# A Fourier mixing stage and routed experts: the final logits matmul as a stream of its own, and block transposes that read the SBUF copy of u one step later

## The chip, the core and the metric

The kernel runs on one core of a Trainium2 chip. The metric is the device time in microseconds of one launch, lower is better. A core has five engines that run side by side, each through its own instructions in program order: TensorE (PE in the profile, with its weight loads as PEld), VectorE (DVE), ScalarE (ACT), GpSimd (POOL) and SyncE (SP), which here issues nearly all DMA transfers. [...] An instruction whose operand is not there yet holds up everything behind it on its engine.

## The reference

Two blocks follow each other. The first is a mixing of 8 sequences of 2496 tokens with 256 channels in frequency space; the second sends each of the 19968 tokens to the one of 8 experts with the largest logit.

```python
X = np.fft.rfft(x, axis=1)                     # x: (8, 2496, 256)
y = np.fft.irfft(X * (filt_r + 1j * filt_i)[None], n=2496, axis=1)

x = y.reshape(19968, 256)
logits = x @ w_gate                            # (256, 8)
expert_idx = np.argmax(logits, axis=1)
probs = np.exp(logits - logits.max(-1, keepdims=True))
probs /= probs.sum(-1, keepdims=True) + 1e-09
gate_w = probs[np.arange(N), expert_idx]
# for each expert e, over its tokens:
h = np.maximum(x_e @ w1[e], 0.0)               # (256, 1024)
y_e = h @ w2[e]                                # (1024, 256)
out = gate_w[:, None] * y
```

## The kernel before, in words

**The transform.** 2496 = 39 x 64, so the transform of a sequence (a "batch" here) is taken as a two-dimensional one, by matmuls with tables. Of the 39 frequencies along the first axis 20 are kept, as real and imaginary parts. There are four stages. Stage A (line 361) takes the 39-point transform of `x` into `zd` in DRAM. Stage B (line 375) takes the 64-point transform; VectorE multiplies its product by the filter (lines 382 to 384) and adds the two halves (line 388 on GpSimd or 391 on VectorE). Stage C (line 401) takes the inverse 64-point transform, giving `u`, which goes to `ud` in DRAM. Stage D (line 423) takes the inverse 39-point one, giving the tokens `yo`. Stages A and D run in six chunks of up to four columns, B and C in ten pairs of frequencies. Between the stages the data are rearranged by the trip through DRAM: the stores are `zd<-zo` and `ud<-uo`, the loads `fin<-zd` (line 346), `fin<-ud` (line 353) and `fin<-in_x` (line 341). A load takes one of seven `fin` buffers.

**The logits.** They are taken from `u`, ahead of stage D, since stage D acts on another axis than the gate. In before, stage C's product in PSUM is read twice: a copy to SBUF (`uo`, line 402, on VectorE or ScalarE) for the trip through DRAM, and a transpose of 32 x 32 blocks on VectorE (line 406) into `tu`. For each of two halves of the frequencies (12 and 8) `u_logits` multiplies `tu` by the gate (line 525, 32 small matmuls), and `turn_logits` turns the result (line 551) and stores it to `vd` in DRAM in four pieces. After the second half `load_logits` brings it back into `spec` in six pieces (line 566), and `logits` applies the last 39-point transform to it (line 575). Only after this matmul does the routing of the batch start: `route` works out expert and row of each token on VectorE, `send_rows` scatters the tokens' rows to DRAM by GpSimd, and `tile_map` finds which tile of rows belongs to which expert. The first batch takes another way through on-chip transposes and has no trip of its logits through DRAM.

**The experts.** Tiles of 512, 256 or 128 rows of one expert are loaded (`xg<-rows`, line 775, and `ng`, 779), turned on VectorE (line 814), multiplied by `w1` (line 857 in a form that saves an eighth of the products, line 898 plainly) and by `w2` (line 915), and scattered to the output (line 921). The weights `w1t` and `w2t` are loaded in halves of 512 KB (lines 808 and 804). Row number and expert are read by SP from values that VectorE wrote.

**What sets the order.** PE, VectorE, ScalarE and SP stand in an order that the Python code works out itself. `slot(k)` lists the steps of a time slot: stages B and C of batch k, stage A of batch k + 1, stage D and the routing of batch k - 1. Each step is a tuple of a due time as a share of the slot, the function, the data that it needs, a charge in microseconds of PE, and a stream: "b", "a" or "d". The main loop keeps a clock, `now`, moved on by the charges. It takes the first step of the list; if that one's data are reckoned to be late by this clock (`lands`), it looks among the next 16 steps for the first ready one, but passes over every step of a stream of which an earlier step has been passed over. Between steps of the transform it gives out expert work, by a credit. After each step the stores noted one step earlier are issued (`flush`), delayed loads whose time has come are issued, and further loads follow (`more_loads`, `prefetch`). The clock only orders the instructions; on the chip each engine waits for its semaphores.

For the last logits matmul the clock works so: `turn_logits` of the second half sets the load to 5.0 after `now`, `load_logits` reckons the landing at 7.0 after the issue, and `logits(k - 1)` is a step of stream "d", ahead of the six chunks of stage D of that batch.

```python
delayed.append((now[0] + 5.0, lambda: load_logits(b)))          # line 557
lands["v", b] = now[0] + 7.0                                    # line 570
steps.append((at - 0.04, lambda: logits(k - 1), ("v", k - 1), 0.3, "d"))   # line 967
```

`free["v"]` and `free["s"]` are the planner's guess of when VectorE and ScalarE come free; `either` sends a copy to the one that would be done first.

Of the kernel before, what the change touches and what calls it, by code (L numbers as in the profile page):

```python
# [10 lines left out]
F32 = mybir.dt.float32  # L11
# [8 lines left out]
P = 128  # L20
S = 2496
D = 256
# [98 lines left out]
def kernel(  # L121
# [16 lines left out]
    nc = tc.nc  # L138
# [9 lines left out]
    for b in range(B):  # L148
        GROUPS.append([])
        for rows, most in WANT[b]:  # L150
            n = min(most, max(0, ((b + 1) * S - (N - left) - E * (rows - 1)) // rows))
# [32 lines left out]
    sb = fft.enter_context(tc.tile_pool(name="sb", bufs=2))  # L184
# [38 lines left out]
    now = [0.0]  # L223
# [22 lines left out]
    HALVES = [(0, 12), (12, NF - 12)]  # L246
# [121 lines left out]
    def stage_b(b, f):  # L368
        c, j = divmod(f, 4)
        if b == 0:  # L370
            zi, j = outs.pop(("zi", f)), 0
        else:
            zi = ins["z", b, c] if j == 0 else ins.pop(("z", b, c))
        p = bank()
        mm(p, lhsT=tbs, rhs=zi[:, j:j + 2, :], start=True, stop=True)  # L375

        z2 = p.rearrange("p (i d) -> p i d", i=2)
        ys = outs["y", b, f] = sb.tile([P, 2, D], F32, tag="ys", name="ys", bufs=4)
        yw = (pro if b == 0 else sb).tile([P, 2, D], F32, tag="yw", name="yw", bufs=2)
        half, f1 = divmod(f, NF // 2)  # L380
        fi = ht[half * HP:(half + 1) * HP, NF + f1:NF + f1 + 2, :]
        nc.vector.tensor_mul(ys, z2, ht[:, f:f + 2, :])  # L382
        nc.vector.scalar_tensor_tensor(out=yw[:HP], in0=z2[HP:], scalar=-1.0, in1=fi, op0=ALU.mult, op1=ALU.mult)
        nc.vector.tensor_mul(yw[HP:], z2[:HP], fi)
        free["v"] = max(free["v"], now[0]) + 2.1

        if b == 0 or b < 3 and not sides:
            nc.gpsimd.tensor_tensor(ys, ys, yw, op=ALU.add)
            free["p"] = max(free["p"], free["v"]) + (1.4 if b else 0.0)
        else:  # L390
            nc.vector.tensor_tensor(ys, ys, yw, op=ALU.add)
            free["v"] += 0.7

    def stage_c(b, f):
        ys = outs.pop(("y", b, f))
        j = f % 4
        if j == 0:
            outs["u", b] = sb.tile([P, 4, D], F32, tag="st", name="uo", bufs=4)
        uo = outs["u", b]
        p = bank()  # L400
        mm(p, lhsT=tcs, rhs=ys, start=True, stop=True)  # L401
        evac(uo[:, j:j + 2, :], p.rearrange("p (i d) -> p i d", i=2), 512)
        f0, n = HALVES[f >= HALVES[0][1]]
        if f == f0:
            outs["t", b] = sb.tile([P, HALVES[0][1], D], F32, tag="tu", name="tu", bufs=1)
        nc.vector.transpose(outs["t", b][:, f - f0:f - f0 + 2, :].rearrange("p i d -> p (i d)"), p)  # L406
        free["v"] = max(free["v"], now[0]) + 0.7
        if j == 2:
            f0 = f - 2
            move(ud[b][:, f0:f0 + 4, :], uo[:HP])  # L410
            move(ud[b][:, NF + f0:NF + f0 + 4, :], uo[HP:])
        if f == NF - 2:
            mark(("c", b))
# [116 lines left out]
    def turn_logits(b, half=0):  # L530
        ls = outs.pop(("l", b))
        if b == 0:
            for i0, m in ((0, 4), (4, 2)):
                pt = bank().rearrange("p (i w) -> p i w", i=4)
                for i in range(m):
                    nc.tensor.transpose(pt[:TK, i, :], ls[:, i0 + i, :], ident)
                pv = pt[:TK].rearrange("p i (g c) -> p i g c", g=4)
                for i in range(m):
                    c = 4 * (i0 + i)
                    w = min(4, NG - c)  # L540
                    whole = min(w, NG - 1 - c)
                    evac(spec[0][:, c:c + whole], pv[:, i, :whole, :E], 8 * whole)
                    if whole < w:
                        evac(spec[0][:NS, c + whole:c + w], pv[:NS, i, whole:w, :E], 8)
            lands["v", b] = now[0]
            return
        f0, n = HALVES[half]
        w = n // 4 * CT
        pt = bank()[:w, :P]
        vt = sb.tile([HALVES[0][1] // 4 * CT, P], F32, tag="vt", name="vt", bufs=1)[:w]  # L550
        nc.tensor.transpose(pt, ls, ident)
        evac(vt, pt, P)
        for m in range(4):
            move(vd[b][m, f0:f0 + n].rearrange("(g k) r e -> (k r) g e", g=4),
                 vt.rearrange("p (g m e) -> p m g e", g=4, m=4)[:, m])
        if half:
            delayed.append((now[0] + 5.0, lambda: load_logits(b)))

    def load_logits(b):
        for th in range(2):  # L560
            of = vd[b][2 * th:2 * th + 2].rearrange("c f r e -> (c f) r e")
            for j in range(NB):
                i0 = -((j - th * HT) // NB) if th else 0
                t0 = NB * i0 + j - th * HT
                n = (HT - 1 - t0) // NB + 1
                nc.sync.dma_start(
                    out=spec[b % 2][j * NS:(j + 1) * NS, i0:i0 + n],
                    in_=of[:, t0:t0 + NB * (n - 1) + 1:NB, :],
                )
        lands["v", b] = now[0] + 7.0  # L570

    def logits(b):
        lgs[b] = sb.tile([TP, NG, E], F32, tag="lg", name="lg", bufs=1)
        p = bank()[:TP, :NG * E]
        mm(p, lhsT=tds, rhs=spec[b % 2].rearrange("p i e -> p (i e)"), start=True, stop=True)
        evac(lgs[b].rearrange("p i e -> p (i e)"), p, NG * E)
        sides.append(route(b))
# [355 lines left out]
    def slot(k):  # L933

        steps, nch = [], len(CH)
        if k == 0:
            steps.append((0.4, load_rest, None, 0.0, None))
            for f in range(-2, NF + 2, 2):
                at = (f + 2) / (NF + 4)
                if 0 <= f < NF:  # L940
                    steps.append((at, lambda f=f: stage_b(k, f), None, 0.85, "b"))
                if f + 2 < NF:
                    steps.append((at + 0.01, lambda f=f: turn_z(f + 2), None, 0.44, "b"))
                if f >= 2:
                    steps.append((at + 0.02, lambda f=f: first_c(f - 2), None, 0.85, "b"))
        elif k < B:
            for f in range(0, NF + 4, 2):
                at = f / (NF + 4)
                if f < NF:
                    steps.append((at, lambda f=f: stage_b(k, f), ("z", k, f // 4) if f % 4 == 0 else None, 0.85, "b"))  # L950
                if f >= 4:
                    steps.append((at + 0.01, lambda f=f: stage_c(k, f - 4), None, 0.85, "b"))
            for half, (f0, n) in enumerate(HALVES):
                at = (f0 + n + 4) / (NF + 4) + 0.005
                steps.append((at, lambda half=half: u_logits(k, half), None, 2.6 if half == 0 else 2.1, "b"))
                steps.append((at + 0.04, lambda half=half: turn_logits(k, half), None, 0.2, "b"))
        if k + 1 < B:
            for c in range(nch):
                steps.append(((0.25 if k == 0 else 0.0) + 0.7 * c / nch, lambda c=c: stage_a(k + 1, c), ("x", k + 1, c), 0.43 * CH[c][1], "a"))
        if k > 0:  # L960
            for c in range(nch + 1):
                at = 0.8 * c / (nch + 3) - 0.1 if k == 1 else (0.35 if k == 2 else 0.2) + 0.8 * c / (nch + 3)
                if c == 0:
                    if k == 1:
                        steps.append((at - 0.07, lambda: u_logits(k - 1), None, 4.4, "d"))
                        steps.append((at - 0.06, lambda: turn_logits(k - 1), None, 0.7, "d"))
                    steps.append((at - 0.04, lambda: logits(k - 1), ("v", k - 1), 0.3, "d"))
                if c < nch and k == 1:
                    steps.append((at - 0.05, lambda c=c: turn_u(c), None, 0.22 * CH[c][1], "d"))
                if c < nch:  # L970
                    steps.append((at, lambda c=c: stage_d(k - 1, c), ("u", k - 1, c) if k > 1 else "y", 0.43 * CH[c][1], "d"))
                    steps.append((at + 0.02, lambda c=c: sides.append(send_rows(k - 1, c)), None, 0.0, "d"))
                if k == 1 and c == nch:
                    steps.append((at, experts_pool, None, 0.0, "d"))
            steps.append((0.73 if k == 1 else 2.0, lambda: begin_route(k - 1), None, 0.0, "d"))
        return sorted(steps, key=lambda step: step[0])
# [249 lines left out]
```

## Time and profile before

| what | us |
|---|---|
| median of three runs | 1525.34 (1522.54 to 1527.35) |
| the profiled execution | 1525.43 |
| its span, first to last instruction | 1523.7 |
| PE busy | 1430.0 |
| PE weight loads busy | 1131.9 |
| VectorE busy | 741.5 |
| GpSimd busy | 702.4 |
| ScalarE busy | 444.3 |
| data moved | 278.01 MB, 182 GB/s in the mean |

The profile was taken in one execution. In it busy times are unions of an engine's instructions; the difference to the span is time in which the engine waited. In lists of waits a line reads: engine, what it was about to do, what it waited for, then the total in us, how often, and the longest. In windows the columns are the stretch, then for PE, PEld, DVE, ACT and POOL the busy us with the number of instructions, then the granted clock of TensorE, the mean busy share of the 16 DMA engines, and GB/s. In a timeline a line is start, duration, engine, source line, operation, what is written and read, and how many are merged, with the idle time before it in brackets. A matmul of the program shows as two records. Groups of instructions end with busy us, mean ns of one, and the engine's idle time before them with what ended it. SPq is SP's queue, in which a DMA shows with the time that its issue took.

### The profile page before, as it was taken

What the parts mean: (1) busy time and instruction counts of PE and PEld (TensorE: products, weight loads), DVE (VectorE), ACT (ScalarE), POOL (GpSimd) and SP (SyncE); (2) the same over time, 40 slices, a digit from 0 to 9 for tenths busy, and PEclk for the clock granted to TensorE, in tenths of its full rate; (3) what the DMA queues carried; (4) which work ended last, traced back from release to release, by engine and by line L of the source; (5) the groups of instructions that cost most, each with busy time, mean ns of one, the idle gap of its engine ahead of it and who ended that gap; (6) DMA issues with size and microseconds to landing.
All of it is one profiled execution on the core that took longest, in us unless ns stands there. A gap on an engine that the chain in (4) does not pass through costs nothing. (4 is left out here: it accounts for less than half of the span.)

```text
span 1523.7 us, 23874 instructions
## 1 busy us (share of the span) xinstructions
PE 1430.0 (94%) x7354; PEld 1131.9 (74%) x7354; DVE 741.5 (49%) x1479; ACT 444.3 (29%) x870; POOL 702.4 (46%) x911
## 2 busy tenths in 40 slices
PE   7986967999999997999989996999999999999998
PEld 5533525766777776777857885788888889999997
DVE  4684675264766555555577454446525343440000
ACT  3531422233232222222212222222222222224332
POOL 3351616325445641566427543566455546741111
PEclk9997988999999998999999998999999999999999
DMA  9788988889877648765486437453655453455661
GB/s 222 195 245 237 270 216 270 232 222 325 230 197 216 188 138 195 190 182 162 129 174 191 132 116 179 116 157 96 207 171 189 144 174 103 119 188 171 186 185 40
DMA packets 253416, 278.01 MB, mean 182 GB/s; under 512 B 162471, under 2 KB 200752, under 8 KB 253289
## 3 DMA queue, kind: packets, MB, share of 16 engines
q1 hardware_dynamic: 234169, 233.13, 56.0%
q0 software_dynamic: 19120, 43.33, 8.5%
q8 instruction: 62, 1.02, 0.3%
q14 instruction: 65, 0.53, 0.1%
HBM read 195.80 MB, written 81.22 MB: 182 GB/s over the span
## 5 line engine op out<-in xcount | busy, mean ns | idle before, releaser
L915 PE MATMUL bank<-w2t,hT 128*128 128x256 f32 x1984 | 443.7, 381 | 0.4 <-ACT hT L870 0.4
L861 DVE TENSOR_TENSOR hT<-bank,hT 128x512 f32<-128x512 f32 (+1 forms) x504 | 298.9, 626 | 283.2 <-PE bank L857 189.3
L915 PEld LDWEIGHTS bank<-w2t,hT 128*128 128x128 f32 x1984 | 378.1, 191 | 69.2 <-issue 15.0
L921 POOL DMA_INDIRECT out_dram<-ys,ng x161 | 160.4, 996 | 479.3 <-DMA out_dram<-ys,ng 138.1
L865 ACT ACTIVATE hT<-hT 128x1024 f32<-128x1024 f32 (+1 forms) x144 | 131.9, 955 | 340.0 <-DVE hT L861 340.0
L681 POOL DMA_INDIRECT rows<-yo,row x176 | 179.4, 1019 | 76.5 <-issue 46.7
L857 PE MATMUL bank<-xT,w1t 128*128 128x256 f32 (+1 forms) x864 | 190.0, 356 | 0.0
L920 ACT ACTIVATE ys<-bank,ng 128x256 f32<-128x256 f32 x136 | 64.3, 473 | 407.5 <-PE bank L915 324.0
L857 PEld LDWEIGHTS bank<-xT,w1t 128*128 128x128 f32 x864 | 152.3, 190 | 25.2 <-issue 6.5
L857 PE MATMUL bank<-sums,wsum 128*128 128x256 f32 (+1 forms) x576 | 135.1, 357 | 1.1 <-POOL sums L821 0.8
L915 PE MATMUL bank<-w2s,hT 128*128 x592 | 132.6, 379 | 0.0
L898 PEld LDWEIGHTS bank<-xT,w1t 128*128 128x128 f32 x864 | 116.1, 193 | 18.9 <-issue 12.5
L898 PE MATMUL bank<-xT,w1t 128*128 128x128 f32 (+1 forms) x864 | 125.8, 301 | 2.7 <-DVE xT L814 2.7
L814 DVE STREAM_TRANSPOSE xT<-xg 128x512 f32<-128x512 f32 (+2 forms) x126 | 57.4, 493 | 142.0 <-PE bank L898 122.4
L915 PEld LDWEIGHTS bank<-w2s,hT 128*128 128x128 f32 x592 | 110.3, 190 | 13.8
L857 PEld LDWEIGHTS bank<-sums,wsum 128*128 128x128 f32 x576 | 101.4, 190 | 23.9 <-issue 9.9
L382 DVE TENSOR_TENSOR ys<-bank,ht 128x512 f32<-128x512 f32 x80 | 54.7, 684 | 91.5 <-PE bank L375 91.1
L361 PE MATMUL bank<-fin,tas 117*120 117x512 f32 x154 | 76.9, 620 | 10.8 <-DMA fin<-in_x_dram 10.8
L832 POOL TENSOR_TENSOR wsum<-w1t 128x256 f32<-128x256 f32 x72 | 53.5, 744 | 69.2 <-PE bank L857 44.4
L904 ACT ACTIVATE hT<-bank 128x128 f32<-128x128 f32 (+1 forms) x209 | 62.6, 300 | 55.0 <-PE bank L898 49.8
L401 PE MATMUL bank<-ys,tcs 128*128 128x512 f32 x140 | 73.5, 611 | 4.9 <-DVE ef L726 3.1
L406 DVE STREAM_TRANSPOSE tu<-bank 128x512 f32<-128x512 f32 x70 | 49.4, 709 | 57.1 <-ACT uo L238 56.6
(157 smaller groups left out, 1496.3 us busy)
## 6 DMA issues: line engine op xcount, KB each, us to landing
w1t<-in_moe_w_dram SPq DMA_DIRECT2D x126, 512.0 KB
w2t<-in_moe_w_dram SPq DMA_DIRECT2D x68, 512.0 KB
fin<-in_x_dram SPq DMA_DIRECT2D x39, 512.0 KB
fin<-zd SPq DMA_DIRECT2D x70, 256.0 KB
ud<-uo SPq DMA_DIRECT2D x70, 256.0 KB
zd<-zo SPq DMA_DIRECT2D x35, 480.0 KB
fin<-ud SPq DMA_DIRECT2D x35, 480.0 KB
xg<-rows SPq DMA_DIRECT2D x112, 128.0 KB
```

The source lines that it names most:

```text
L361: mm(p[:TK, :], lhsT=tas, rhs=xt[:TP, j:j + 2, :], start=True, stop=True)
L401: mm(p, lhsT=tcs, rhs=ys, start=True, stop=True)
L681: sc = nc.gpsimd.indirect_dma_start(out=rowsd, out_offset=bass.IndirectOffsetOnAxis(ap=at, axis=0), in_=what, in_offset=None,)
L814: nc.vector.transpose(xts[i][:, dh, :n * P].rearrange("p (g r) -> p g r", r=QW), xg[:, :n * NQ, dh, :])
L857: mm(q[:, v], lhsT=left[:, v * P:(v + 1) * P], rhs=right, start=True, stop=True)
L861: nc.vector.tensor_tensor(o, q, a, op=ALU.add)
L865: nc.scalar.activation(o.rearrange("p v r c -> p v (r c)"), q.rearrange("p v r c -> p v (r c)"), AF.Relu)
L898: mm(p[:, :m], lhsT=w1t[2 * i + g][:, dh, fh, v * P:(v + 1) * P], rhs=xts[i][:, dh, :m], start=(dh == 0), stop=(dh == DH - 1))
L904: lambda: nc.scalar.activation(hT, p[:, :m], AF.Relu))
L915: mm(p[:, :D], lhsT=hs[i][k % 4 // 2][:, k // 4, k % 2, j * P:(j + 1) * P], rhs=w2, start=(k == 0), stop=(k == FT - 1))
L920: lambda: nc.scalar.activation(ys, p[:, :D], AF.Copy, scale=gate))
L921: nc.gpsimd.indirect_dma_start(out=out, out_offset=bass.IndirectOffsetOnAxis(ap=gis[i].bitcast(U32)[:, j, :1], axis=0), in_=ys, in_offset= ...
```

## The change

Three things are changed.

Stage C no longer transposes its product out of PSUM. It notes the pair of frequencies in a list, and a new function, `turn_u_blocks`, transposes what is on the list from `uo` in SBUF. It is called by the next stage C before its matmul, by stage B between its products and its add, and as a step of its own shortly before each `u_logits`.

The charges of `u_logits` in the planner are lowered: 2.6 and 2.1 to 1.5 and 1.1 for the two halves, and 4.4 to 2.4 for the first batch.

The final logits matmul becomes stream "l", so that a passed-over `logits` doesn't keep back stage D; its load is delayed by 6.0 instead of 5.0, and its landing is reckoned at 10.0 instead of 7.0 after the issue.

```diff
@@ stage_b
         nc.vector.tensor_mul(yw[HP:], z2[:HP], fi)
+        turn_u_blocks()
         free["v"] = max(free["v"], now[0]) + 2.1
@@
+    turns = []
+
+    def turn_u_blocks():
+
+        for b, f, u in turns:
+            f0, n = HALVES[f >= HALVES[0][1]]
+            if f == f0:
+                outs["t", b] = sb.tile([P, HALVES[0][1], D], F32, tag="tu", name="tu", bufs=1)
+            nc.vector.transpose(outs["t", b][:, f - f0:f - f0 + 2, :].rearrange("p i d -> p (i d)"),
+                                u.rearrange("p i d -> p (i d)"))
+            free["v"] = max(free["v"], now[0]) + 0.6
+        turns.clear()
+
     def stage_c(b, f):
         ys = outs.pop(("y", b, f))
+        turn_u_blocks()
         j = f % 4
...
         evac(uo[:, j:j + 2, :], p.rearrange("p (i d) -> p i d", i=2), 512)
-        f0, n = HALVES[f >= HALVES[0][1]]
-        if f == f0:
-            outs["t", b] = sb.tile([P, HALVES[0][1], D], F32, tag="tu", name="tu", bufs=1)
-        nc.vector.transpose(outs["t", b][:, f - f0:f - f0 + 2, :].rearrange("p i d -> p (i d)"), p)
-        free["v"] = max(free["v"], now[0]) + 0.7
+        turns.append((b, f, uo[:, j:j + 2, :]))
@@ turn_logits
         if half:
-            delayed.append((now[0] + 5.0, lambda: load_logits(b)))
+            delayed.append((now[0] + 6.0, lambda: load_logits(b)))
@@ load_logits
-        lands["v", b] = now[0] + 7.0
+        lands["v", b] = now[0] + 10.0
@@ slot
-                steps.append((at, lambda half=half: u_logits(k, half), None, 2.6 if half == 0 else 2.1, "b"))
+                steps.append((at - 0.03, turn_u_blocks, None, 0.0, "b"))
+                steps.append((at, lambda half=half: u_logits(k, half), None, 1.5 if half == 0 else 1.1, "b"))
@@
-                        steps.append((at - 0.07, lambda: u_logits(k - 1), None, 4.4, "d"))
+                        steps.append((at - 0.07, lambda: u_logits(k - 1), None, 2.4, "d"))
                         steps.append((at - 0.06, lambda: turn_logits(k - 1), None, 0.7, "d"))
-                    steps.append((at - 0.04, lambda: logits(k - 1), ("v", k - 1), 0.3, "d"))
+                    steps.append((at - 0.04, lambda: logits(k - 1), ("v", k - 1), 0.3, "l"))
```

## The prediction

> **What bounds the kernel now.** I read the page first (part 1), then the waits of the PE queue, then the windows, and last the timelines of PE and SP around the longest waits.
>
> ```profile
> PE 1430.0 (94%) x7354; PEld 1131.9 (74%) x7354; DVE 741.5 (49%) x1479; ACT 444.3 (29%) x870; POOL 702.4 (46%) x911
> 1050.00:1100.00 50.00, 50.00 (x233) 44.03 (x232) 29.44 (x61) 12.28 (x17) 25.06 (x32) 1.00 0.54 163
> 1450.00:1500.00 50.00, 50.00 (x346) 47.11 (x345) 3.94 (x16) 19.27 (x65) 7.20 (x8) 1.00 0.51 151
> PE bank L575 <- DMA spec<-vd: 40.8, 7, 12.4
> PE bank L361 <- DMA fin<-in_x_dram: 10.8, 2, 9.2
> PE lt L525 <- DVE tu L406: 4.6, 5, 2.3
> ```
>
> PE is busy 94% of the span, and from 1050 us on without a gap (50.00 of 50 in each window up to 1500): the last third is matmuls alone. So a microsecond of PE idleness that goes before 1050 comes off the end, and one that is added lengthens it. The gaps of PE above 0.15 us add up to 87 us. Almost half, 40.8, stands before one instruction, the final logits matmul L575, seven times, each waiting for `spec` to come back from DRAM. Next is stage A waiting for `x` (10.8). VectorE is at 49% and PE waits for its transposes 4.6 us in all.
>
> What such a wait looks like on PE, for batch 2:
>
> ```profile
> 200.72 1.10 PE L401 MATMUL bank<-ys,tcs 128*128 128x512 f32 x2 [0.23 <-DVE ef L726]
> 211.74 0.91 PE L575 MATMUL bank<-spec,tds 120*117 120x176 f32 x2 [9.92 <-DMA spec<-vd]
> 212.44 3.62 PE L423 MATMUL bank<-fin,tds 120*117 120x512 f32 x4
> 218.35 1.88 PE L423 MATMUL bank<-fin,tds 120*117 120x512 f32 x4
> 236.26 3.74 PE L361 MATMUL bank<-fin,tas 117*120 117x512 f32 x4 [9.15 <-DMA fin<-in_x_dram]
> ```
>
> and on SP's queue at the same time:
>
> ```profile
> 198.72 2.61 SPq L320 DMA_DIRECT2D vd<-vt  x4
> 206.65 3.49 SPq L566 DMA_DIRECT2D spec<-vd  x6
> 221.27 2.26 SPq L775 DMA_DIRECT2D xg<-rows  x4
> 228.88 1.62 SPq L341 DMA_DIRECT2D fin<-in_x_dram  x1
> 200.00:210.00 10.00, 1.59 (x4) 0.30 (x2) 9.13 (x41) 0.84 (x2) 0.00 (x0) 0.69 0.98 227
> ```
>
> The reader should see three things. PE stands in program order, so with L575 at its head nothing behind it runs. The wait costs more than itself: the four L423 after it take 3.62 us, four a little later 1.88, so 1.7 us is lost to a half clock. And the last line has the DMA share at 0.98 (last but one number) with PE busy 1.59 of 10 us: here the transfers themselves are the limit, and the `x` that stage A wants at 227 was issued only at 228.88, behind the experts' rows and weights.
>
> [...]
>
> **The change part by part.**
>
> (a) Transposes from SBUF, a step later. The same 70 instructions; from PSUM 709 ns, and the transpose of equal shape from SBUF (L814) 683 ns:
>
> ```profile
> L406 DVE STREAM_TRANSPOSE tu<-bank 128x512 f32<-128x512 f32 x70 | 49.4, 709 | 57.1 <-ACT uo L238 56.6
> L814 DVE STREAM_TRANSPOSE xT<-xg 128x512 f32<-128x512 f32 x56 | 36.2, 683 | 0.0
> ```
>
> 70 x 26 ns = 1.8 us of VectorE, and most of its 56.6 us of waiting for ACT's copy goes, since that copy is done a step later. But VectorE is no bound: PE's waits for it are a few us. A PSUM bank is given back earlier; no PE wait is for a bank. On the other side `uo` is read longer, but its store to `ud` is issued two steps late anyway and holds it as long. The transpose now stands before the add L391 and delays that product by 0.7 us; stage C follows four frequencies later, which hides it. The last transpose of a half still comes right before L525, which waits as before. Cost 0; bounds -5 us (all waits of L525 gone) and +3 (the add late at some C).
>
> (b) Charges of `u_logits` in the planner: 2.6 and 2.1 become 1.5 and 1.1, and 4.4 becomes 2.4. L525 takes 11.0/7 = 1.57 and 10.6/7 = 1.51 us in the trace, so the planner's clock comes nearer to PE's. No instruction changes; only the order.
>
> (c) Load of the logits at +6 instead of +5, their landing reckoned 10 after it instead of 7, and L575 in a stream "l", so that stage D no longer stands behind it. What it does can be read in the order of the built programs. PE's instructions are the same 4211, in another order. I count the PE work that stands between the second turning of the logits (L551) and L575, at 0.86 us for a 512-column matmul and 0.43 for a 256-column one (start to start in the timeline, two records each). Per batch, stall before; cover before and after:
>
> ```
> batch   1     2     3     4     5     6     7
> stall   6.0   9.9   0.3   0.3   7.3   4.6   12.4
> before  14.8  8.8   15.7  20.9  17.4  15.7  8.0
> after   16.6  10.5  19.1  20.9  20.9  14.0  11.4
> ```
>
> From L551 to the landing of `spec` before took 16 to 29 us, and most of that is SP's queue, which issues in order: four stores of `vd`, one or two blocks of experts' rows (each waits for a row number, then about 2.5 us of issues), `z` loads, then six loads of `spec`. Where SP's order is unchanged the gain is the added cover, up to the stall.
>
> Batch 1: cover +1.8. The `vd` stores now stand ahead of the rows and weights (they were issued at 133.3, with `vt` ready at 123.3), one `zd` store more stands before `spec`; issue about 1 us earlier. Gain 2.8.
> Batch 3: 0.3. Batch 4: 0. Batch 5: same SP order, 3.5.
> Batch 6: cover -1.7; a weight load less ahead and the tile map on VectorE a little earlier, about +0.7. Loss 1.
> Batch 7: cover +3.4, and one rows block instead of two ahead of `spec`:
>
> ```profile
> 933.42 6.56 SPq L320 DMA_DIRECT2D vd<-vt  x4
> 941.05 2.02 SPq L775 DMA_DIRECT2D xg<-rows  x4
> 944.54 2.26 SPq L775 DMA_DIRECT2D xg<-rows  x4
> 947.44 3.81 SPq L566 DMA_DIRECT2D spec<-vd  x6
> ```
>
> The first block's last issue (`ng`, 943.26 + 0.41) ends at 943.7, so without the second `spec` could go 947.4 - 943.7 = 3.7 us earlier, unless the last `vd` store has not landed (batch 2 shows 5.3 us from the end of those issues at 201.3 to 206.6). Gain 5.5 to 7; I take 7.
>
> Batch 2, with its neighbourhood: cover +1.7 at L575. But an `x` load (512 KB), a `ud` load (480) and a `zd` store (480) now stand ahead of `spec`: 1.47 MB, at the 227 GB/s of this stretch 6.5 us if all of it is served first, nothing if the loads fit into the hole from 203.5 to 206.6[...]. What comes after is better ordered: the next `x` is issued right after `spec`, before the rows and weights, so at about 216 (a slot of `fin` comes free with the first stage D after L575) instead of 228.9. So the 9.15 us wait goes. Next late is `z` for stage B, which now stands behind the rows and weights: these took from 211 to 226 before, so it is issued near 229, lands near 235 (6 us like `x` at 228.9 to 236.3), where PE comes to that B at 228. Before, B started there at 242.85. Gain 235 against 242.85 = 8, less what `spec` slips (0 to 6.5): 2 to 8, I take 5, and 1.7 for the clock that isn't lost a second time.
>
> Sum: 2.8 + 0.3 + 0 + 3.5 - 1 + 7 + 5 + 1.7 = 19.3 us.
>
> (d) What is shortened elsewhere. Lead of loads in the new order, counted in PE work from issue to use: one `w2` pair (512 KB each, tile 3, near 290 us) falls from 21 to 8, one `x` chunk from 12.8 to 10.7. Two of 512 KB take about 4.5 us at 227 GB/s and the SP issue; a wait of 0 to 3 us. For this and for DMA shares of 0.8 to 0.98 up to 450 us, where a faster PE meets data that isn't there yet, I take 4 off (0 to 12). That leaves 15.
>
> The profiled execution took 1525.43 us, with a span of 1523.7; the median of three is 1525.34, so nothing has to be shifted. 1525.4 - 15 = 1510.5.
>
> **Rivals.**
> 1. More is won: `spec` lands where PE reaches L575, because the planner's loads drift apart from the rows blocks, and the `x` waits go with it. For it: all seven waits are of one kind. Ceiling 40.8 + 9.2 + six half-clock stretches of 1.7 = 60. Against: SP's order keeps the rows ahead of `spec` in six batches. Some 30 us, 1495.
> 2. Only moved: up to 450 us the bytes are the limit, and batches 1 and 2 give nothing; batch 7 waits for the landing of `vd`, 3.4 alone. Then 3.5 + 3.4 - 1 = 6, less the 4 of (d): 1523.5.
> 3. Slower, by SP's order in batch 2: `spec` lands 6.5 us later behind 1.47 MB, everything after it on SP slips by as much, `z` for stage B comes at 242 and the weights of the next tiles with it, and the shorter lead of `w2` turns into waits. Price 6.5 - 1.7 at L575, about 7 at B without the old `x` wait's 9 to pay for it, and repeated waits of 5 to 7 us for experts' weights over three tiles: 25 lost against 11 won in batches 1, 5, 6 and 7. 1536. It decides once the stretch from 190 to 300 us takes over 11 us more than before. For it: the share of 0.98. Against: the bytes are the same, and the same window runs PE at 100% from 250 on with the share at 0.80.
> That the transposes matter (a) is no rival of weight: its bounds are inside the range.
>
> **How the numbers follow.** Forecast 0.50, rival 1 0.12, rival 2 0.14, rival 3 0.24. The forecast's own range is 1503 to 1518. To leave no more than 2 in 10 out I go from 1498 to 1531. About 0.3% (4.6 us) is what a measurement of this kernel can tell from no change. Faster: forecast and rival 1, 0.62. Within: rival 2, 0.14. Slower: 0.24.
>
> **What would show it.** The wait of L575 near 25 to 30 us in place of 40.8, below 8 in batch 7 and near 4 in batch 5, larger in batch 6. The 9 us wait of L361 gone and one of L375 on `zd` in its place near 235. L406's wait for ACT gone with VectorE's busy time unchanged. PE still without a gap in the last third. I am wrong if L575's waits sum as before, if new waits of L915 or L857 on weights exceed 5 us, or if the stretch 190 to 300 got longer.

## The result, and the profile after

The changed kernel takes 1541.2 us (median of four) against 1526.34 for before on the same chip: ratio 1.0098, 95% interval 1.0075 to 1.0121. I had forecast 1510.5. It is slower by 15 us where I expected it to be faster by 15, and the time lies outside my range. Its profiled execution took 1541.23 us with a span of 1539.4. All ratios here are of undisturbed executions; one of the five of k4_ac_hold took 3848 us and is left out.

The busy times of the changed kernel, from the page:

```profile
PE 1436.3 (93%) x7354; PEld 1136.1 (74%) x7354; DVE 734.2 (48%) x1477; ACT 445.0 (29%) x871; POOL 704.0 (46%) x912
```

Its longest waits on PE (engine and what it was about to do, what it waited for, then total us, times, longest). Its line numbers are 11 higher from stage D on: L586 is the final logits matmul, L926 the product with `w2`, L536 the small logits matmuls.

```profile
PE bank L586 <- DMA spec<-vd: 39.8, 6, 12.5
PE bank L375 <- DMA fin<-zd: 9.6, 2, 8.4
PE bank L926 <- DMA w2t<-in_moe_w_dram: 6.7, 2, 5.8
PE lt L536 <- DVE tu L403: 6.0, 8, 1.7
PE bank L361 <- DMA fin<-in_x_dram: 2.7, 2, 1.9
```

The waits for `spec`, which the change was to shorten, are 39.8 us where they were 40.8. The wait for `x` went from 10.8 to 2.7, and one for `zd` of 9.6 stands in its place. The one for `w2`, 6.7, is new. All gaps of PE above 0.15 us sum to 96.1 us instead of 86.9. That is 9.2 of the 15.7 us of span; 6.3 more are PE's busy time, 1436.3 against 1430.0, for the same 7354 records.

To see where the time went I lay the two traces side by side by work done: each matmul record counts with the usual distance from start to start of its kind in before, and what a stretch took beyond that is lost, be it a gap or matmuls at a lower granted clock (in before it was 0.50 from 211.7 to 217 us, behind the wait of batch 2, and 1.00 from 218 on). The table gives the loss in us for stretches of equal work; the two orders differ by a few us within a stretch.

```
stretch (time in before)                          before  after
start to 187 us                                   difference +0.9
batch 2: logits, x or z wait (187 to 249)           30.4   34.2
wsum of the next tile                                0      2.0
second half of batch 3's logits (293 to 311)         5.9    6.0
w2 of the fourth tile (after: 338 to 354)            0      8.4
small waits, 367 to 426                              4.2    3.6
batch 4's logits                                     0      4.3
batch 5                                             12.3    9.4
batch 6                                             12.8   20.0
batch 7                                             18.9   11.2
```

So batches 5 and 7 won 10.6, and batches 2, 4, 6, the weights, their sums (`wsum`) and the start lost some 27. From there on nothing changes: PE runs without a gap in both (busy 450.00 of 450 us from 1050 to 1500 in before, and as much from 1060 to 1510 in the changed kernel, at a granted clock of 1.00).

Batch 2 in the changed kernel, PE's timeline (start, duration, instruction, how many records, gap before it):

```profile
216.55 0.91 PE L586 MATMUL bank<-spec,tds 120*117 120x176 f32 x2 [11.57 <-DMA spec<-vd]
217.25 6.25 PE L434 MATMUL bank<-fin,tds 120*117 120x512 f32 x8
232.52 1.88 PE L434 MATMUL bank<-fin,tds 120*117 120x512 f32 x4
242.82 2.05 PE L375 MATMUL bank<-fin,tbs 128*128 128x512 f32 x2 [8.42 <-DMA fin<-zd]
```

and SP's queue in the same stretch:

```profile
207.74 7.18 SPq L577 DMA_DIRECT2D spec<-vd  x6
216.90 1.84 SPq L341 DMA_DIRECT2D fin<-in_x_dram  x1
234.64 0.49 SPq L346 DMA_DIRECT2D fin<-zd  x1
```

The six loads of `spec` took 7.18 us to issue, 3.49 before, and PE got them at 216.55 instead of 211.74. With L586 next in its order, PE was busy 0.00 us from 205 to 216.5, and from there to 222 its granted clock was 0.50. The next `x` was issued early, as foreseen, and its wait is gone. But the `z` load behind the rows and weights went out at 234.64 instead of the 229 that I had reckoned, and stage B started at 242.82. Before it started, with the same work done, at 242.85: nothing was won.

Batch 6, SP's queue before, with PE's line:

```profile
766.27 2.62 SPq L320 DMA_DIRECT2D vd<-vt  x4
774.14 1.95 SPq L775 DMA_DIRECT2D xg<-rows  x4
782.50 4.66 SPq L566 DMA_DIRECT2D spec<-vd  x6
788.75 0.91 PE L575 MATMUL bank<-spec,tds 120*117 120x176 f32 x2 [4.58 <-DMA spec<-vd]
```

and after:

```profile
782.87 6.64 SPq L320 DMA_DIRECT2D vd<-vt  x4
791.10 3.79 SPq L786 DMA_DIRECT2D xg<-rows  x4
800.14 3.74 SPq L577 DMA_DIRECT2D spec<-vd  x6
```

with PE's line:

```profile
805.37 0.91 PE L586 MATMUL bank<-spec,tds 120*117 120x176 f32 x2 [12.49 <-DMA spec<-vd]
```

The logits were turned at 764.82 before and at 777.59 after. So the stores of `vd` start 5.3 us after that instead of 1.5, they take 6.64 us instead of 2.62, and the issue of `spec` begins 22.6 us after the turning instead of 17.7, with 1.7 us less PE work ordered ahead of the matmul: 12.49 us of waiting instead of 4.58.

The same view for all batches, worked out from the traces: from the start of the turning (L551) to the end of the last `spec` issue, and the wait of the logits matmul.

```
batch              1     2     3     4     5     6     7
issued, before     27.5  17.7  14.4  19.6  23.1  22.3  18.9
issued, after      28.3  21.6  13.5  22.2  23.7  26.3  15.0
wait, before       6.0   9.9   0.3   0.3   7.3   4.6   12.4
wait, after        3.2   11.6  0.0   2.6   4.6   12.5  5.3
```

Wherever the matmul waited, in both kernels, it started 1.5 to 2.0 us after the last `spec` issue had ended. So its start follows SP's queue.

### The profile page after: what moved, and what is told of

It reads as the page before. It is cut to its first block, busy times and chain, and to the rows that moved or that the text cites. A ratio compares the mean times of both kernels' runs of the same rounds, so it can differ in the third digit from the quotient of the medians.

```text
span 1539.4 us, 23890 instructions
## 1 busy us (share of the span) xinstructions
PE 1436.3 (93%) x7354; PEld 1136.1 (74%) x7354; DVE 734.2 (48%) x1477; ACT 445.0 (29%) x871; POOL 704.0 (46%) x912
## 5 line engine op out<-in xcount | busy, mean ns | idle before, releaser
L926 PE MATMUL bank<-w2t,hT 128*128 128x256 f32 x1984 | 446.4, 382 | 6.7 <-DMA w2t<-in_moe_w_dram 6.7
L926 PEld LDWEIGHTS bank<-w2t,hT 128*128 128x128 f32 x1984 | 380.1, 192 | 79.7 <-issue 24.4
L926 PE MATMUL bank<-w2s,hT 128*128 x592 | 132.6, 379 | 0.0
L926 PEld LDWEIGHTS bank<-w2s,hT 128*128 128x128 f32 x592 | 110.3, 190 | 13.8
L868 PEld LDWEIGHTS bank<-sums,wsum 128*128 128x128 f32 x576 | 101.3, 190 | 24.8 <-issue 10.6
L375 PE MATMUL bank<-fin,tbs 128*128 128x512 f32 x140 | 73.7, 613 | 9.6 <-DMA fin<-zd 9.6
```

What stands on the lines that cost most here:

```text
L868: mm(q[:, v], lhsT=left[:, v * P:(v + 1) * P], rhs=right, start=True, stop=True)
L926: mm(p[:, :D], lhsT=hs[i][k % 4 // 2][:, k // 4, k % 2, j * P:(j + 1) * P], rhs=w2, start=(k == 0), stop=(k == FT - 1))
```

## The experiments

My theory after the result: the order decides, and in it the race between the work ahead of the logits matmul (cover) and the landing of `spec`, which is set by what stands ahead on SP. The rivals: the transposes cost in themselves; the later load costs; any shift of the order costs. First each part of the change alone, and a shift that means nothing.

**e1_turn: the transposes alone**, with the books of before, given out by the next stage B or C and, at the latest, inside `u_logits`. PE's order is that of before.

```diff
-        nc.vector.transpose(outs["t", b][:, f - f0:f - f0 + 2, :].rearrange("p i d -> p (i d)"), p)
+        turns.append((b, f, uo[:, j:j + 2, :]))
 def u_logits(b, half=0):
+        turn_u_blocks()
         n = HALVES[half][1] // 4
```

> Part (a) alone: the transposes read uo in SBUF a step later; the planner's books and the steps are left as in before, so that PE, SP and ScalarE stand in the order of before. Theory (order and leads): the loss lies in parts (b) and (c), so 1526 +- 3, with L406's wait for ACT gone and PE's waits for tu between 2 and 7 us. Rival (the SBUF read or the later transpose itself costs): 1531 to 1541, with the growth in waits of stage C for the add and of the logits' matmuls for tu.

1535.0 us, ratio 1.0066 (1.0041 to 1.0092). By the time the rival was right. The waits point to the place of the transposes:

```profile
PE bank L586 <- DMA spec<-vd: 25.6, 5, 12.1
PE lt L536 <- DVE tu L402: 15.4, 11, 3.0
```

The waits for `tu` rose from 4.6 to 15.4 us. (At L586 7.7 us more are put down to `fin<-ud`, so that matmul waits 33.3 in all, less than before.) My reading is that a transpose given out only with the logits matmul stands on VectorE behind the expert work given out in between. The change avoids this by a step of its own, so this run is not yet its part (a); the next one is.

**a1_turn_steps: the transposes as the change has them**, with the step at 0.03 ahead; charges, load, landing and stream as before.

> Part (a) alone as the change has it, with its step ahead of each logits matmul and 0.6 in the planner; charges, load and landing as in before. SP's order is all but that of before, PE's differs in batch 2, where a chunk of stage A moves ahead of the final logits matmul (cover 10.5 instead of 8.8). Theory (what e1_turn lost was its place, 11 us of waits for tu where the transposes were given out only with the logits matmul): waits for tu 4 to 8 us, 1522 to 1530. Rival (the deferred SBUF transposes cost in themselves): waits for tu above 12 us, 1533 or more.

1528.3 us, ratio 1.0018 (0.9998 to 1.0039): no difference that can be told.

```profile
PE lt L536 <- DVE tu L403: 6.2, 7, 1.7
```

The transposes are not the cause. Their group in the changed kernel:

```profile
L403 DVE STREAM_TRANSPOSE tu<-uo 128x512 f32<-128x512 f32 x70 | 49.3, 707 | 24.2 <-ACT uo L238 22.7
```

The mean is 707 ns from SBUF here, 709 from PSUM in before.

**e2_charge: the charges alone.**

```diff
-  u_logits(k, half), None, 2.6 if half == 0 else 2.1, "b"
+  u_logits(k, half), None, 1.5 if half == 0 else 1.1, "b"
-  u_logits(k - 1), None, 4.4, "d"
+  u_logits(k - 1), None, 2.4, "d"
```

> Part (b) alone: charges 1.5, 1.1 and 2.4. In the resulting order two pairs of w2 have leads of 7.9 and 8.8 us (before: none below 8.6, one there), batches 3 and 6 lose 1.7 and 2.6 us of cover before the logits matmul, batches 5 and 7 win 3.5 and 2.5. Theory (order and leads): a wait of 4 to 8 us for w2 between 280 and 360 us, a larger logits wait in batch 6; 1529 to 1536. Rival (the charges only make the clock truer, the loss is in the later load of the logits): 1526 or less.

1541.89 us, ratio 1.0109 (1.0081 to 1.0137): the whole loss of the change. The waits are not where I said:

```profile
PE bank L575 <- DMA spec<-vd: 51.0, 7, 15.7
PE bank L361 <- DMA fin<-in_x_dram: 14.6, 1, 14.6
```

PE waits 1.2 us for `w2` in all, and none of it between 280 and 360 us, although the order shortens its lead as in the changed kernel. The waits for `spec` rise by 10.2 us; batch 6 alone waits 15.7, with the last `spec` issue ending 28.7 us after the turning instead of 22.3.

**k3_halves: only the charges of the two halves.** The three runs named with a k were on another chip, on which before takes 1552.58 us; only their ratios are compared.

> In before only the charges of the two halves are lowered (2.6 and 2.1 to 1.5 and 1.1), 4.4 stays. Covers exactly those of e2_charge (14.8, 8.8, 14.0, 20.9, 20.9, 13.1, 10.5), and SP's order in batch 1 as there. Theory: all of e2_charge's loss is theirs, 1537 to 1546. Rival (4.4 to 2.4 has a share): 1525 to 1532.

Ratio 1.0101 (1.0066 to 1.0136): these two charges, lowered by 2.1 us together in each slot, make the loss.

**e3_stream: load, landing and stream alone.**

```diff
-  delayed.append((now[0] + 5.0, lambda: load_logits(b)))
+  delayed.append((now[0] + 6.0, lambda: load_logits(b)))
-  lands["v", b] = now[0] + 7.0
+  lands["v", b] = now[0] + 10.0
-  logits(k - 1), ("v", k - 1), 0.3, "d"
+  logits(k - 1), ("v", k - 1), 0.3, "l"
```

> Part (c) alone: load at +6, landing at +10, stream l. Covers rise by 1.8, 0, 1.7, 0, 3.5, 1.7, 3.4 us in batches 1 to 7; an x load, a ud load and a zd store stand ahead of spec in batch 2; no lead of w2 shrinks. Theory (order and leads): batch 2's stretch from 190 to 260 us loses about 6, the other covers win about 9, no wait for w2: 1520 to 1527. Rival (part c is what costs): 1532 or more.

1526.82 us, ratio 1.0015 (0.9996 to 1.0034).

```profile
PE bank L575 <- DMA spec<-vd: 42.3, 7, 14.2
```

Cover rose in five batches, by 12.1 us in sum, and over the seven batches the last `spec` issue came 12.1 us later in sum, so nothing was won (batch 2 waits 14.2, batch 6 8.8). The stream has no part in it: with "d" in its place, here and in the changed kernel, the program is the same instruction for instruction. Stage D finds no moment in which it could pass.

**k1_ac: the changed kernel with the old charges,** and the final logits matmul in stream d.

> The changed kernel with the old charges (2.6, 2.1, 4.4) and the logits matmul in stream d, that is parts (a) and (c) without (b). Covers as in the changed kernel in batches 1 to 5 and 7, 17.4 instead of 14.0 in batch 6; no pair of w2 with a lead below 9. Theory (the charges cost, by the order that they make: the w2 wait near 345 us and batch 6): no wait for w2, batch 6 waits 5 to 9 us instead of 12.5, 1520 to 1530. Rival (the parts cost only together): 1535 or more.

Ratio 0.9967 (0.9950 to 0.9984): faster than before. Parts (a) and (c) together win 0.3%, and the charges turn that into a loss of 1%. Its longest waits have no `w2` near 345 us; that for `spec` is 29.9 (there is no trace of before from this chip to set beside it):

```profile
PE bank L586 <- DMA spec<-vd: 29.9, 5, 9.3
PE bank L926 <- DMA w2t<-in_moe_w_dram: 1.8, 1, 1.8
```

**e4_null, n3_before_null, n1_after_null: shifts that mean nothing.** The two charges of before lowered by 0.1, raised by 0.1, and those of the changed kernel lowered by 0.1.

> A change that means nothing: in before the charges 2.6 and 2.1 become 2.5 and 2.0. The order shifts nevertheless: cover of batch 3 -1.7, of batch 4 +1.7, of batch 6 -2.6, of batch 7 +0.8. Theory (order and leads): batch 6's wait grows by about 3, 1526 to 1531. Rival (before is a tuned optimum of the order, any shift costs about 1%): 1536 or more.

> In before the charges 2.7 and 2.2 instead of 2.6 and 2.1. Covers 14.0, 19.1, 20.9 instead of 15.7, 20.9, 17.4 in batches 3 to 5. Theory (leads and covers): 1522 to 1528. Rival (before is a good draw among orders): 1530 or more, as e4_null.

> The changed kernel with a shift that means nothing: charges 1.4 and 1.0 instead of 1.5 and 1.1. Covers as after but 13.1 instead of 11.4 in batch 7. Theory (leads and covers): 1537 to 1541, the same w2 wait near 345 us. Rival (the time of an order is as good as drawn by lot, some 10 us to either side): anywhere from 1520 to 1555, by waits at other places.

Ratios 1.0153 (1.0125 to 1.0181), 1.0023 (1.0008 to 1.0037) and 1.0102 (1.0037 to 1.0167; two executions alone, 1547.1 and 1535.13 us). A tenth of a microsecond, twice in a slot, costs 1.5% when it is taken off, more than the whole change, and 0.2% when it is added. So the cost does not grow with the size of the lowering. Nor is before a single lucky order: a1_turn_steps, e3_stream, k1_ac and n3_before_null have other orders of PE and charges of 2.6 or 2.7 for the first half, and their ratios are 0.9967 to 1.0023, while all four with charges of 2.5 or less (e4_null, e2_charge, k3_halves, n1_after_null) and the changed kernel itself are at 1.0098 to 1.0153. Charges between 1.5 and 2.5, or well above 2.7, were not tried. In e4_null too the loss shows at the logits matmul:

```profile
PE bank L575 <- DMA spec<-vd: 47.3, 5, 15.3
PE bank L575 <- DMA fin<-ud: 11.6, 1, 11.6
```

That is 58.9 us in all, 18.1 more than before. (The second line is the same matmul; the profile names another load that landed last.)

**h1_hold: SP's order alone.** In before, experts' rows are not loaded while a load of the logits is outstanding. PE's order is that of before.

```diff
-  rows_at[work[i][3]] <= now[0] and i - used["x"] < 2:
+  rows_at[work[i][3]] <= now[0] and i - used["x"] < 2 and not delayed:
```

> In before, no block of experts' rows is loaded while a load of the logits is outstanding, so spec is issued ahead of the rows blocks in batches 4 to 7; PE stands in the order of before (covers 14.8, 8.8, 15.7, 20.9, 17.4, 15.7, 8.0 us). Theory (the landing of spec is set by what stands ahead of it on SP): from the logits' turning to the landing 13 to 17 us instead of 21 to 25 in these batches, the waits of batches 5 and 6 gone, that of batch 7 near 6; 20 us less wait for spec, less up to 5 for rows that come later: 1506 to 1515. Rival (the landing is set by the stores of vd or by the DMA queues): waits as before, 1523 or more.

1514.24 us, ratio 0.9923 (0.9896 to 0.9950). SP's queue in batch 5, first in before, then with the hold:

```profile
583.89 2.91 SPq L320 DMA_DIRECT2D vd<-vt  x4
587.91 3.88 SPq L775 DMA_DIRECT2D xg<-rows  x4
594.48 2.10 SPq L775 DMA_DIRECT2D xg<-rows  x4
597.81 4.45 SPq L566 DMA_DIRECT2D spec<-vd  x6
```

```profile
581.98 2.61 SPq L320 DMA_DIRECT2D vd<-vt  x4
590.69 2.92 SPq L566 DMA_DIRECT2D spec<-vd  x6
594.97 1.95 SPq L775 DMA_DIRECT2D xg<-rows  x4
```

`spec` now goes ahead of the rows; the last issue ends 16.5 us after the turning (23.1 before) and the wait of batch 5 is 0.6 us (7.3). The waits of the logits matmul, short ones included, sum to 22.0 us instead of 40.8: 19 us less, of which 11 reach the end. In batches 4 to 7 the last issue ends 4.9 to 7.0 us earlier after the turning. Since PE's order is the same, this shows that in these batches the landing was set by SP's order. The waits, with those that came instead:

```profile
PE bank L575 <- DMA spec<-vd: 11.3, 2, 7.5
PE bank L575 <- DMA fin<-ud: 10.1, 1, 10.1
PE bank L361 <- DMA fin<-in_x_dram: 12.1, 2, 11.5
PE bank L857 <- POOL wsum L833: 9.1, 3, 7.4
```

The wait for `x` was 10.8 before. The last line is new: GpSimd's weight sums come late.

**h2_hold_cover: the same, and much more cover** (landing reckoned at 17, and the matmul in stream l).

> As h1_hold, and the landing reckoned at 17 instead of 7 after the load: covers 24.3, 8.8, 25.2, 24.3, 24.3, 24.3, 19.1 us. Theory (cover against landing): no wait for spec but in batch 2 (10), total below 14: 1495 to 1510. Rival (any shift of the order brings its own new waits, on x, z, u and w2, of 10 to 20 us): waits for spec as small, but 1515 to 1535.

1539.04 us, ratio 1.0087 (1.0055 to 1.0118): the rival was right in kind, and the loss is larger than it said.

```profile
PE bank L857 <- POOL wsum L833: 19.9, 3, 8.9
PE bank L575 <- DMA fin<-ud: 14.8, 1, 14.8
PE bank L915 <- DMA w2t<-in_moe_w_dram: 14.4, 4, 6.4
```

The logits matmul waits in batch 2 alone. But 34 us of waits for `wsum` and `w2` have come in. My reading is that later logits mean later routing and scatters on GpSimd; the trace shows it for one of these waits, where four scatters (464.84 to 469.79 us) and an output scatter (471.00 to 472.01) stand right ahead of the weight sums that PE waits for at 473 us. Cover was not to be had for nothing here.

**h6_hold_turn, h8_hold_null, h3d_after_hold, k4_ac_hold: the hold on other orders**: on a1_turn_steps, on e4_null, on the changed kernel (with the matmul in stream d), on k1_ac.

> a1_turn_steps with the hold of h1_hold: no block of rows is loaded while a load of the logits is outstanding. Theory: the hold wins what it won in before, 8 to 13 us, whatever the transposes do: 1511 to 1519. Rival (h1_hold was a lucky order): 1523 or more.

> e4_null with the hold (charges 2.5 and 2.0). e4_null waited 47.3 us for spec and once more 11.6 at the same matmul, and took 1548.7. Theory (most of what a shift of the order costs is the same race between cover and landing): waits for spec in batches 3 to 6 gone, 1515 to 1528. Rival (shifts cost through other waits): 1535 or more.

> The changed kernel with the hold, and the final logits matmul in stream d as in before (which leaves the order of the changed kernel as it is; with stream l and the hold the planner comes to a standstill). Covers 19.1, 14.0, 29.5, 20.9, 20.9, 17.4, 10.5 us. Theory (in the changed kernel spec landed later by about as much as cover was added, and the landing is SP's order): the waits of batches 4 to 6 gone, total of waits for spec below 20 us instead of 39.8, time 1520 to 1532; what stays over before are the waits for w2, x and z up to 450 us. Rival (the added loss is elsewhere altogether): waits for spec fall but the time stays at 1536 or more.

> k1_ac with the hold of h1_hold. Theory (cover is worth its microseconds once spec is issued ahead of the rows blocks): waits for spec in batches 4 to 7 near 3 us in all, 1508 to 1517, as good as h1_hold or better. Rival (later logits cost by what hangs on them, the routing and GpSimd's scatters, as in h2_hold_cover): 1520 or more, with waits for wsum and w2 above 10 us.

Ratios to before: 0.9937 (0.9915 to 0.9959), 1.0079 (1.0057 to 1.0101), 1.0022 (0.9994 to 1.0050), 0.9878 (0.9834 to 0.9922). Against the same kernel without the hold (1.0018, 1.0153, 1.0098, 0.9967) it wins 0.7 to 0.9% each time. So the race at the logits matmul is real, and in the changed kernel it is worth 0.8%, though there, and a little in k4_ac_hold, the hold also moves PE's order.

But the hold doesn't lessen what the charges cost, and this goes against my theory. h3d_after_hold and k4_ac_hold differ in the charges alone, and their ratios are 1.5% apart; without the hold the same pair, the changed kernel and k1_ac, is 1.3% apart. For the shift by a tenth (e4_null and h8_hold_null, whose order on PE is the same) it is 1.5% without the hold and 1.6% with it. So rows ahead of `spec` cost the kernels with the old and with the new charges alike, and are not what the new charges brought.

The waits for `spec` in h3d_after_hold are 8.3 us, yet it is no faster than before:

```profile
PE bank L361 <- DMA fin<-in_x_dram: 18.9, 3, 16.6
PE bank L909 <- DVE xT L825: 10.2, 1, 10.2
PE bank L586 <- DMA spec<-vd: 8.3, 3, 3.6
```

Its order brings waits for `x` and for turned rows up to 250 us instead. h8_hold_null missed my expectation by 10 us: its batch 6 still waits 8.8 us for `spec`, and 9.5 us of waits for `wsum` have come in. Parts (a) and (c) with the old charges and the hold, k4_ac_hold, has the lowest ratio of all, 1.2% faster than before, with 14.6 us of waits for `spec` where k1_ac has 29.9. Whether its cover adds something to the hold can't be told, since its interval and that of h1_hold overlap.

## Why the prediction was wrong

**Part (a), cost 0:** right (1.0018). The 26 ns that I took from another transpose's row are not there (707 against 709 ns). VectorE's wait for ACT's copy fell from 56.6 to 22.7 us, and PE gained nothing by it, as said.

**Part (b), "no instruction changes; only the order":** this is the step that failed. I gave the charges no price of their own and read the new order as if it could only do what my table of covers and my few leads of loads said. Measured alone they cost 1.1%, and without them the change is faster than before by 0.3%. That gives the sign. It doesn't give the whole miss, since I had forecast 1%: the rest is part (c).

**Part (c), "where SP's order is unchanged the gain is the added cover":** near in batch 5 (wait -2.7, forecast 3.5). In batch 7 the reckoning with one rows block less was right too (-7.1, forecast 7). In batch 1 the number was right by luck (-2.8, forecast 2.8): `spec` was issued not 1 us earlier after the turning but 0.8 later, and PE's other waits in between, longer by 2.0 us, covered it. As a rule the sentence is wrong, since it takes the landing of before as fixed. In batch 4, with SP's order from the stores to `spec` and the cover unchanged, the stores began 2.0 us later after the turning, the issue of `spec` ended 2.6 later, and the wait grew by 2.3. In batch 6 I had the loss as 1 and it was 7.9: cover -1.7 as counted, but the `vd` stores began 3.8 us later and took 4 us more to issue. I had assumed a gain of 0.7 there. In e3_stream, part (c) alone, such slips ate all of the 12.1 us of added cover.

**Batch 2's neighbourhood, 5 plus 1.7:** measured -3.8. The slip of `spec` was 4.8 us, inside my 0 to 6.5, but not in the way that I reckoned, by bytes served first. All of it is in the issue, which began 1.1 us later and took 3.7 longer (7.18 against 3.49); from its end to the matmul it is 1.6 us in both kernels. Why the issue was longer no run here shows. Nor was 227 GB/s a limit of the transfers, as I had read it: the same stretch, 200 to 210 us, moved 292 GB/s in the changed kernel. Next, the `z` load came at 234.64 instead of 229, mostly because SP was slipped by those 4.8 us. My rival 3 had this mechanism, with 242 for stage B. It was the better forecast in sign and near in size (it says 1536; its own terms, 25 lost against 11 won, make 1539), but not in place: at most 4 of the 15 us were lost here, and of the weights' waits that it foresaw over three tiles there was one.

**Part (d), 0 to 3 for `w2`:** 6.7 us of wait, 8.4 with what the matmuls after it lost (the granted clock was 0.50 from 346 to 348 us). PE's timeline and SP's queue show why:

```profile
346.01 3.37 PE L926 MATMUL bank<-w2t,hT 128*128 128x256 f32 x8 [5.83 <-DMA w2t<-in_moe_w_dram]
333.64 3.72 SPq L577 DMA_DIRECT2D spec<-vd  x6
338.74 1.96 SPq L786 DMA_DIRECT2D xg<-rows  x4
342.15 0.37 SPq L815 DMA_DIRECT2D w2t<-in_moe_w_dram  x1
343.79 0.34 SPq L815 DMA_DIRECT2D w2t<-in_moe_w_dram  x1
```

The two halves stood behind the six `spec` loads, which wait for the stores, and a rows block; PE had reached them at 340 and went on at 346. I priced the lead in PE work, and it was spent on SP. The short lead alone was no cause: e2_charge has two such leads and no such wait. Of the signs that I had named for being wrong all three came: the waits of the logits matmul sum nearly as before, the new wait for `w2` exceeds 5 us, and the stretch from 190 to 300 us got longer.

What stays open: I cannot say from these runs which single step of the reordering makes the charges cost what they cost. The waits move from batch to batch between orders that differ by a tenth of a microsecond. One mark does recur. Counted in PE work at the usual distances, as in the table of stretches, the second turning of batch 3's logits stands 227 to 241 us from the start in every order with lowered charges, and in h2_hold_cover, and 220 to 222 us in all others. The former are the slower ones, each against its counterpart with or without the hold. No run moved that step alone, so it isn't shown to be the cause.

## What to carry to other kernels

Where a planner orders instructions ahead of time, price a change of its charges by runs with charges shifted for no reason; here such shifts of before moved the time by 0.2 and 1.5%, so that a loss of 1% says little about the reason for the change. Take such a change apart, too: two parts of this one were worth 0.3%, and the third lost 1.3%. Cover for a transfer is worth its microseconds only as long as its landing stays where it is (in e3_stream 12.1 us of added cover met issues that ended 12.1 us later): follow the issuing queue first, and move the transfer ahead of what it doesn't need there. When an experiment removes a wait, see whether it removes the loss that you want to explain; here it won as much, 0.7 to 0.9%, in the kernels that didn't have that loss. Delaying a step that starts a chain on other engines (here routing and scatters) can pay its waits back later: that is my reading of the 34 us of waits for `wsum` and `w2` in h2_hold_cover.

## What the runs showed that I had not expected

The issue of small-piece transfers on SP has no fixed length: four stores of `vd` took 2.62 or 6.64 us and six loads of `spec` 3.49 or 7.18 us in the stretches shown, for the same bytes. With PE waiting at the end of the chain, 1.5 to 2.0 us after the last issue, these 4 us count in full. What makes an issue long the runs don't show. And one kernel differs between chips by more than any change here: before took 1525 us on one and 1552.58 on the other, while the loss of the charges was the same on both (1.0109 and 1.0101).
